# Key tiles of the second batch transposed ahead and stored in a conformer kernel

## The chip, the cores and the metric

One core of a Trainium2 chip. The metric is the device time of one execution in microseconds (us); the kernel before is given by the median of three runs.

## The reference

A conformer block over two batches of 4000 tokens with 512 features, in bf16:

```python
h = layernorm(x);  x1 = x + 0.5 * (silu(h @ w_ff1_a) @ w_ff1_b)
h = layernorm(x1); q, k, v = h @ w_q, h @ w_k, h @ w_v
p = softmax(q @ k^T / sqrt(512))              # every token of a batch against all of that batch
x2 = x1 + (p @ v) @ w_o
h = layernorm(x2) @ w_pw1; h = h[..., :D] * sigmoid(h[..., D:])
h = depthwise_conv3(h, dw); h = (h - mean) / sqrt(var + 1e-5)      # over all 8000 tokens
x3 = x2 + silu(h) @ w_pw2
h = layernorm(x3); x4 = x3 + 0.5 * (silu(h @ w_ff2_a) @ w_ff2_b)
return layernorm(x4)
```

## The kernel before

The weights of q and k are folded into one matrix, and v and the output weights into another, so the normalized tokens `h` themselves serve as keys and as values. The first feed-forward stage writes them to the DRAM tensor `keysd`. Attention then reads them in two forms: `self.h[kt]`, a plain copy with 128 tokens on the partitions (for the values), and `self.hT`, the same 128 tokens transposed, with features on the partitions (for the scores). A transposed tile comes from one DMA transpose (`key_queries`). A batch has 32 key tiles (`KT`), of which the last holds the 32 leftover tokens four times (`tailsd`).

`attention` runs 16 groups `g` of up to 512 queries, eight for each batch, and in each group 32 steps `kt`, one for each key tile. The first group of a batch (`g` 0 and 8) computes its scores plainly, tile by tile (`scores`). The other groups take the tiles 2 to 29 in seven quads of four tiles (`score_quad`), with a scheme that multiplies seven half-size products in place of eight; it needs sums of key tiles, made once in the first group of a batch by `k_sums`, stored in `kfd`, and read back in each group by `k_stream` into a pair of buffers. The value products use the same scheme (`pv`), with sums stored in `v12d` and `v4d` and read back by `v_stream`.

Between the two batches the key tiles in SBUF are exchanged while groups 7 and 8 run (`keys_swap`). The value side of it is prepared during groups 1 to 5: every ten steps, `v_ahead` loads two tiles of the second batch into the buffer `vst`, forms sums on VectorE and stores `vst`, `v4d` and `v12d`; `v_back` loads them in group 8. The transposed key tiles come by 32 DMA transposes spread over groups 7 and 8.

The tail tile of 32 tokens is scored by `tail_scores`: sixteen small matmuls into PSUM bank 1, an exponential, a store to `pqd` and four loads into `ptail`, which is read at the start of the next group (`sum_tail`, `pv_rest`). Its step is 9 in all groups but the first. At steps 24 and 28 a pair of convolution products for the group before is made (`pair`, `conv_b`, `conv_a`, `pw1`), whose PSUM bank comes from a ring (`sbank`).

All instructions are recorded first and then ordered for each engine by a planner (`Plan`). It goes through the program in time with costs of its own and takes for each engine, of what is ready, the instruction that is due first; TensorE (PE) may be reordered by at most 8 us of its own work, the other engines run at most 16 us ahead. The result is one fixed list for each engine. All DMAs named here are in the list of SyncE (SP), and an instruction that waits there holds up those behind it. Two instructions that write the same buffer are ordered by it:

```python
def transpose(self, dst, src, reads, writes):
    k = self.S.dsems[16 + self.nxt("tr", 12)]
    return self.S.dma("SP", k, lambda e: e.dma_start_transpose(dst, src), reads=reads, writes=writes)
```

All instructions are recorded through one helper, so in the profile they nearly all have line 93; they are told apart by the tensors that they write and read (`xt<-v12d`). In these names the regions stand: `keys` holds `h` and `hT`, `xt` the residual tiles and the buffers of `kfd` and `v12d`, `wff` the weights and `vst`, `work` queries and small buffers, `sums` the exponentials, `s` and `y` the eight PSUM banks.

Of the kernel before, what the change touches and what calls it, by code (L numbers as in the profile page):

```python
# [6 lines left out]
BF16 = mybir.dt.bfloat16  # L7
# [5 lines left out]
B, T, D, F, KW = 2, 4000, 512, 2048, 3  # L13
# [3 lines left out]
TPC = 4  # L17
# [11 lines left out]
QUADS = 7  # L29
HC, HD, HF = CHUNK // 2, D // 2, FC // 2  # L30
KT = -(-T // 128)
REST = T % 128
DC = D // 128
# [6 lines left out]
def width(c):  # L40

    return CHUNK if c % TCB < TCB - 1 else T - (TCB - 1) * CHUNK
# [11 lines left out]
def tile_rows(c, ti):  # L54

    if c % TCB < TCB - 1 or ti < TPC - 1:
        return slice(0, TILE)
    lo = c // TCB * HALF
    return slice(lo, lo + TAIL)
# [491 lines left out]
class Conformer:  # L551
# [35 lines left out]
    def memory(self):  # L587
        nc = self.nc
# [54 lines left out]
        at = [8192 + t % self.CONV_SLOTS * 4096 if t < self.NBESIDE else 20480 + (t - self.NBESIDE) * 4096  # L643
              for t in range(NCK)]
# [60 lines left out]
        self.hq = A.view(2048, QUADS * 2048).rearrange("p (q u r e j k) -> p q u r e j k", q=QUADS, u=2, r=2, e=2, j=2)  # L705
        self.kfd = nc.dram_tensor("kfd", [B, QUADS, 128, 1536], BF16, kind="Internal").ap()
        self.b_kfd = [[Buf("kfd") for _ in range(QUADS)] for _ in range(B)]
        self.vhd = nc.dram_tensor("vhd", [PAIRS, 128, 2 * D], BF16, kind="Internal").ap()
        self.v4d = nc.dram_tensor("v4d", [PAIRS, 128, HD], BF16, kind="Internal").ap()
        self.v12d = nc.dram_tensor("v12d", [B, PAIRS, 128, 2 * HD], BF16, kind="Internal").ap()  # L710
# [1224 lines left out]
    def v_ahead(self, i, step):  # L1935
# [9 lines left out]
        else:  # L1945
            self.store(self.vhd[i], x, b_x, [self.b_vhd[i]])
            self.store(self.v4d[i], f1, b_1, [self.b_v4d[i]])
            self.store(self.v12d[1][i], f2, b_2, [self.b_v12d[1][i]])

    def v_back(self, j, which):  # L1950
        p = self.group(j)
        i, k = p[0], p[-1] + 1
        if which:
            self.load(self.V4[:, i:k], self.v4d[i:k].rearrange("n p d -> p n d"), self.b_V4[i:k], reads=self.b_v4d[i:k])
        else:
            self.load(self.hv[:, i:k].rearrange("p n k e d -> p n (k e d)"), self.vhd[i:k].rearrange("n p d -> p n d"),
                      self.b_h[2 * i:2 * k], reads=self.b_vhd[i:k])
# [92 lines left out]
    def attention(self, old, hook):  # L2050

        for g in range(NCK):
            W, plain = width(g), g % TCB == 0
            for kt in range(KT):
                if plain:
                    self.ring = [0, 1, 2]
                else:
                    self.ring, self.rings["S"] = list(self.ASIDE.get(kt, (0, 1))), 0
                if plain and kt < KT - 1 or kt < 2 or kt == KT - 2:
                    ps, b_ps = self.scores(g, kt, None if plain else self.bank((0, 2)[kt] if kt < 2 else 0))  # L2060
                    if kt < KT - 2:
                        self.exp_pair(g, kt, ps, b_ps)
                    else:
                        self.act(self.P30[:, 0:W], ps[:, 0:W], AF.Exp, [b_ps], [self.b_P30], scale=SCALE)
                elif not plain and kt < KT - 2:
                    self.score_quad(g, *divmod(kt - 2, 4))
                if g == 0 and kt < 2:
                    self.pop(old // 2 if kt == 0 else old - old // 2)
                if kt == (9 if g else 21):
                    self.tail_scores(g)  # L2070
                if g:
                    self.units_late(g - 1, kt)
                self.units(g, kt)
                self.next_queries(g, kt, 9 if g else 0)
                hook(g, kt)
                self.forms(g, kt)
                self.keys_swap(g, kt)
                self.tick()
# [122 lines left out]
    def keys_swap(self, g, kt):  # L2201

        at = g * KT + kt
        if g == 0:
            steps = [(1, n) for n in range(5)] if kt == 3 else []
            j, r = divmod(kt + 1, 4)
            if 1 < j < GROUPS:
                steps += {0: [(j, 0)], 1: [(j, 1)], 2: [(j, 3)], 3: [(j, 2), (j, 4)]}[r]
            for j, n in steps:
                self.v_here(j, n)  # L2210
            if kt in (26, 27):
                self.v_rest(kt - 26)
        i, r = divmod(at - KT - 4, 10)
        if 0 <= i < PAIRS:
            for n in {0: (0,), 4: (1, 2), 5: (3, 4), 8: (5,)}.get(r, ()):
                self.v_ahead(i, n)
        if TCB - 1 <= g <= TCB:
            at -= (TCB - 1) * KT
            for k in range(KT):
                if (6 + k * (2 * KT - 12) // KT if k < KT - 1 else KT - 12) == at:  # L2220
                    self.key_queries(1, k)
            for j in range(GROUPS):
                if at == KT + 3 + j:
                    self.v_back(j, 0)
                if at == KT + 14 + j:
                    self.v_back(j, 1)
            if at in (KT + 11, KT + 12):
                self.key_values(1, KT - 2 + at - KT - 11)
            if at in (KT + 18, KT + 19):
                self.v_rest(at - KT - 18)  # L2230
# [138 lines left out]
            th, b_th = (self.thl[jj], self.b_thl[jj]) if t == NCK - 1 else (self.thh[k], self.b_th[k])  # L2369
            self.act(th[:, 0:W], ps[:, 0:W], AF.Sigmoid, [b_ps], [b_th])  # L2370

    def conv_a(self, t, jj):

        ps, b_ps = self.pw1(t, jj)
        k, gs, W = jj % 2, t % 2, width(t)
        th = self.th[k][:, 0:W]
        lo = 1 + self.EDGE * (t == NCK - 1)
        out = self.G[gs][:, jj, lo:lo + W]
        wr = [self.b_G[gs][jj], self.b_Gl[gs][jj], self.b_Gr[gs][jj]]
        if t == NCK - 2 and jj >= self.KEEP:  # L2380

            asb, b_asb = self.asb[jj % 3], self.b_asb[jj % 3]
            th = self.thh[k][:, 0:W]
            self.act(asb, ps[:, 0:CHUNK], AF.Copy, [b_ps], [b_asb], scale=2.0)

            def gate(eng):
                ways = {e: lambda e: e.tensor_tensor(out=out, in0=asb, in1=th, op=ALU.mult) for e in (eng, {"DVE": "POOL", "POOL": "DVE"}[eng])}
                self.S.either(ways, [b_asb, self.b_th[k]], wr)
                self.halo_left(t, jj)
                self.halo_right(t, jj)  # L2390

            return gate
        elif t == NCK - 1:
            self.S.op("DVE", lambda e: e.scalar_tensor_tensor(
                out=out, in0=ps[:, 0:W], scalar=2.0, in1=self.thl[jj][:, 0:W], op0=ALU.mult, op1=ALU.mult),
                reads=[b_ps, self.b_thl[jj]], writes=wr)
            return
        else:
            self.S.op("DVE", lambda e: e.scalar_tensor_tensor(
                out=out, in0=th, scalar=1.0, in1=ps[:, 0:W], op0=ALU.add, op1=ALU.mult),  # L2400
                reads=[b_ps, self.b_th[k]], writes=wr)
        self.halo_left(t, jj)
        self.halo_right(t, jj)

    def pw1(self, t, cb):
        ps, b_ps = self.sbank()
        n, W = TPC if width(t) == CHUNK else TPC - 1, width(t)
        if t == NCK - 1:
            moves = [(ps[:, 0:W], self.lin[:, :, 0:W])]
        else:  # L2410
            moves = [(ps[:, 0:n * TILE].rearrange("p (t k) -> p t k", t=n),
                      self.lnT[0][:, 0:n, :, 0:TILE].rearrange("p t c k -> p c t k"))]
            if n < TPC:
                moves.append((ps[:, n * TILE:W], self.lnT[0][:, n, :, tile_rows(t, n)]))
        for out, x in moves:
            for cc in range(DC):
                self.mm(out, self.Wp1[:, cc, cb * 128:(cb + 1) * 128], x[:, cc], cc == 0 and out is moves[0][0], cc == DC - 1,
                        [self.b_Wp1] + self.b_lnT[1 if t == NCK - 1 else 0], b_ps, skip_group_check=True)
        if t < NCK - 1:
            self.touch(ps, b_ps, W)  # L2420
        return ps, b_ps
# [207 lines left out]
    def program(self, any_score):  # L2629
        i = self.i  # L2630
# [99 lines left out]

        tail = NCK - 2

        def pair(t, jj):
            self.conv_b(t, jj)
            self.after(1, lambda: self.conv_a(t, jj))
            if t:
                self.after(3, lambda: self.taps_beside(t - 1, jj))

        here, there = ((22, 27), (3, 8)) if any_score else ((24, 28), (3, 5))

        def att_hook(g, kt):
            if g == 0 and kt == 8:
                self.load(self.Wp1, i["w_pw1"].rearrange("(c p) f -> p c f", p=128), [self.b_Wp1])
            if kt in here and (0 <= g - 1 < tail or g - 1 == tail and here.index(kt) < self.KEEP):
                pair(g - 1, here.index(kt))
            if 0 <= g - 2 < tail and kt in there:
                pair(g - 2, 2 + there.index(kt))
            if g == 0 and self.rest:
# [140 lines left out]
        for k in range(2):  # L2889
            pair = (2 * k, 2 * k + 1)  # L2890
            for ti in pair:
                self.ln_stats(0, sl, ti, x, ((), (), self.b_mv[sl][0:2], self.b_sh[sl][0:2])[ti])
            for ti in pair:
# [4 lines left out]
                 reads=self.b_mv[sl][two] + [self.b_neghalf], writes=self.b_rs[sl][two])  # L2898
# [16 lines left out]
        for ti in all_t:  # L2915
            ps, b_ps = banks[ti]
# [110 lines left out]
```

## Time and profile before

| | |
|---|---|
| median of 3 runs | 1886.56 us (1885.83 to 1886.96) |
| the profiled execution | 1887.44 us, of which its span is 1883.5 us |
| PE busy | 1861.0 us (99%), 15388 matmuls |
| VectorE (DVE) busy | 1485.6 us (79%) |
| ScalarE (ACT) busy | 1336.3 us (71%) |
| GpSimd (POOL) busy | 141.1 us (7%) |
| DMA | 231.50 MB, mean 123 GB/s |
| DMA transposes of keys | 62 from `keysd`, 2 from `tailsd` |

The span runs from the first to the last instruction; what the execution takes beyond it (3.9 us) lies around it. PE busy is the time covered by matmuls, so a gap in it is time in which no matmul was in the array. Attention lies between about 426 and 1400 us of the span.

### The profile page before, as it was taken

The numbers are of one execution on the slowest core, as the hardware profiler recorded it, in microseconds if no ns is written. First come the engines' busy times: TensorE is split into PE (matmuls) and PEld (weight loads), VectorE is DVE, ScalarE is ACT, GpSimd is POOL, SyncE is SP. The second block draws the span as 40 slices with busy tenths as digits, with TensorE's granted clock in tenths as the row PEclk, the third lists the DMA queues.
The fourth block names the chain that finished last, engine by engine and source line by source line (L and its number), as shares of the span: only waits on it lengthen the run. The fifth ranks groups of instructions, "written<-read, shape, count | busy, mean of one in ns | idle before, by whom it ended". The sixth has DMA issues, their size and how long they took to land.

```text
span 1883.5 us, 39160 instructions
## 1 busy us (share of the span) xinstructions
PE 1861.0 (99%) x15388; PEld 1441.9 (77%) x15388; DVE 1485.6 (79%) x3189; ACT 1336.3 (71%) x2421; POOL 141.1 (7%) x301
## 2 busy tenths in 40 slices
PE   9999999999999999999999999999998999999998
PEld 5888888866777777777677777777764888888886
DVE  7889999868668777776777677768768889889885
ACT  5778777755666777777667677777667787777774
POOL 1000000000000000000000000000011000000010
PEclk9999999999999999999999999999999999999999
DMA  7333344196545555348954444444365222221211
GB/s 196 89 85 90 81 113 107 60 271 208 168 142 150 166 167 164 109 127 174 226 149 132 128 124 114 123 137 125 105 197 163 66 59 78 70 55 46 64 32 55
DMA packets 325012, 231.50 MB, mean 123 GB/s; under 512 B 204179, under 2 KB 295638, under 8 KB 324566
## 3 DMA queue, kind: packets, MB, share of 16 engines
q1 hardware_dynamic: 324294, 228.68, 44.4%
q8 instruction: 123, 2.02, 0.4%
q14 instruction: 67, 0.55, 0.1%
q10 hardware_dynamic: 528, 0.26, 0.0%
HBM read 128.44 MB, written 55.79 MB: 98 GB/s over the span
## 4 chain that ended last, share of the span: by engine, by line
PE 93%; ACT 3%; DVE 2%; DMA 1%; issue 0%; SPq 0%; POOL 0%; DVEq 0%; ACTq 0%
PE s L93 47%; PE y L93 46%; ACT work L93 1%; DVE work L93 1%; DMA work<-work 1%; ACT sums L93 1%; ACT xt L93 0%; ACT keys L93 0%; DVE keys L93 0%; DVE wff L93 0%; SPq L93 0%; DVE xt L93 0%; DVE s L93 0%; ACT s L93 0%; DVE sums L93 0%
## 5 line engine op out<-in xcount | busy, mean ns | idle before, releaser
L93 ACT ACTIVATE sums<-s 128x512 bf16<-128x512 f32 (+2 forms) x494 | 287.4, 585 | 158.8 <-PE s L93 157.8
L93 DVE TENSOR_TENSOR sums<-sums 128x512 bf16<-128x512 bf16 (+3 forms) x528 | 201.8, 400 | 102.2 <-ACT sums L93 90.8
L93 ACT ACTIVATE keys<-s 128x512 bf16<-128x512 f32 (+2 forms) x284 | 165.3, 587 | 140.4 <-PE s L93 114.5
L93 PE MATMUL y<-work,keys 128*128 128x256 bf16 x1920 | 244.7, 273 | 0.0
L93 PE MATMUL s<-work,keys 128*128 128x256 bf16 (+5 forms) x1456 | 225.2, 292 | 0.4 <-ACT sums L93 0.3
L93 ACT ACTIVATE work<-xt,work 128x512 bf16<-128x512 bf16 x268 | 202.7, 785 | 10.2 <-DVE work L93 8.5
L93 PE MATMUL y<-wff,keys 128*128 128x256 bf16 (+3 forms) x1592 | 209.2, 276 | 0.1
L93 PEld LDWEIGHTS y<-work,keys 128*128 128x128 bf16 x1920 | 187.9, 98 | 25.1
L93 PE MATMUL y<-sums,keys 128*128 128x256 bf16 (+1 forms) x1440 | 202.1, 270 | 0.0
L93 PE MATMUL s<-sums 128*128 128x256 bf16 x1296 | 194.4, 273 | 0.0
L93 DVE TENSOR_TENSOR keys<-keys 128x1024 bf16<-128x1024 bf16 (+2 forms) x262 | 170.0, 663 | 25.8 <-ACT keys L93 20.4
L93 PE MATMUL y<-work,wff 128*128 128x256 bf16 (+2 forms) x1116 | 184.0, 292 | 0.0
L93 PEld LDWEIGHTS y<-wff,keys 128*128 128x128 bf16 (+1 forms) x1592 | 151.2, 98 | 32.4 <-issue 3.3
L93 DVE BATCH_NORM_STATS2 work<-xt 128x6 f32<-128x512 bf16 x251 | 165.9, 682 | 4.5 <-DMA xt<-in_x_dram 3.8
L93 PEld LDWEIGHTS y<-sums,keys 128*128 128x128 bf16 x1440 | 139.3, 98 | 24.5 <-DVE sums L93 0.3
L93 PEld LDWEIGHTS s<-work,keys 128*128 128x128 bf16 (+1 forms) x1456 | 119.4, 97 | 47.8 <-issue 4.7
L93 POOL TENSOR_TENSOR work<-work 128x4 f32<-128x4 f32 (+3 forms) x107 | 92.0, 862 | 808.4 <-DVE work L93 806.0
L93 PE MATMUL y<-sums,xt 128*128 128x256 bf16 (+1 forms) x960 | 139.7, 270 | 2.6 <-DMA xt<-v12d 1.9
L93 PEld LDWEIGHTS s<-sums 128*128 128x128 bf16 x1296 | 126.7, 98 | 20.0
L93 PE MATMUL s<-work,wff 128*128 128x512 bf16 (+5 forms) x668 | 140.2, 345 | 1.7 <-ACT work L93 1.1
L93 PE MATMUL s<-work 128*128 128x512 bf16 (+4 forms) x565 | 137.9, 374 | 2.4 <-DVE work L93 1.7
L93 PEld LDWEIGHTS y<-work,wff 128*128 128x128 bf16 x1116 | 108.2, 98 | 29.7
(144 smaller groups left out, 3217.4 us busy)
## 6 DMA issues: line engine op xcount, KB each, us to landing
xt<-kfd SPq DMA_DIRECT2D x98, 384.0 KB, 3.2
xt<-v12d SPq DMA_DIRECT2D x105, 256.0 KB, 3.1
xd<-xt SPq DMA_DIRECT2D x28, 512.0 KB, 3.4
xt<-xd SPq DMA_DIRECT2D x28, 512.0 KB, 4.1
out_dram<-xt SPq DMA_DIRECT2D x14, 512.0 KB, 2.9
xt<-in_x_dram SPq DMA_DIRECT2D x13, 512.0 KB, 4.1
dcvd<-wff SPq DMA_DIRECT2D x48, 128.0 KB, 2.0
keys<-dcvd SPq DMA_DIRECT2D x12, 512.0 KB, 3.8
```

Of the source, the lines that this page charges most:

```text
L93: return getattr(eng, self.name)(*self.args, **self.kw)
```

## The change

Fourteen pairs of the second batch's key tiles (the tiles 2 to 29, the seven quads) are transposed ahead. In groups 1 to 5, after each of the first fourteen rounds of `v_ahead`, two DMA transposes write into the same buffer `vst`, and a store puts it into a new DRAM tensor `khd`. In groups 7 and 8 `k_back` brings each pair back by one plain load. The tiles 0, 1, 30 and 31 are still transposed in groups 7 and 8, the last of them later than before. The sums and stores of `v_ahead` move to earlier steps of their round of ten. `tail_scores` moves from step 9 to step 24 in all groups but the first, and `conv_a` at step 24 is given bank 1.

```diff
         self.b_kfd = [[Buf("kfd") for _ in range(QUADS)] for _ in range(B)]
+        self.khd = nc.dram_tensor("khd", [2 * QUADS, 128, 2 * D], BF16, kind="Internal").ap()
+        self.b_khd = [Buf("khd") for _ in range(2 * QUADS)]
...
+    def k_ahead(self, i, step):
+
+        if step == 0:
+            for r in range(2):
+                src, rd = self.key_source(1, self.quad_tiles(i // 2)[2 * (i % 2) + r])
+                self.transpose(self.vst[:, r * D:(r + 1) * D].rearrange("p (c k) -> p c k", c=DC), src, rd, [self.b_vst])
+        else:
+            self.store(self.khd[i], self.vst, [self.b_vst], [self.b_khd[i]])
+
+    def k_back(self, i):
+        k = self.quad_tiles(i // 2)[2 * (i % 2)]
+        b = [self.b_hT[t // TPC][t % TPC] for t in (k, k + 1)]
+        q, u = divmod(i, 2)
+        self.load(self.hq[:, q, u].rearrange("p r e j k -> p (r e j k)"), self.khd[i], b, reads=[self.b_khd[i]])
...
-                if kt == (9 if g else 21):
+                if kt == (24 if g else 21):
                     self.tail_scores(g)
...
         i, r = divmod(at - KT - 4, 10)
         if 0 <= i < PAIRS:
-            for n in {0: (0,), 4: (1, 2), 5: (3, 4), 8: (5,)}.get(r, ()):
+            for n in {0: (0,), 2: (1, 2), 3: (3, 4), 5: (5,)}.get(r, ()):
                 self.v_ahead(i, n)
+            if i < 2 * QUADS and r in (6, 9):
+                self.k_ahead(i, r - 6)
...
-                if (6 + k * (2 * KT - 12) // KT if k < KT - 1 else KT - 12) == at:
-                    self.key_queries(1, k)
+                if (6 + k * (2 * KT - 12) // KT if k < KT - 1 else KT + 6) == at:
+                    if k < 2 or k > KT - 3:
+                        self.key_queries(1, k)
+                    elif k % 2:
+                        self.k_back((k - 2) // 2)
...
-    def conv_a(self, t, jj):
+    def conv_a(self, t, jj, bank=None):
 
-        ps, b_ps = self.pw1(t, jj)
+        ps, b_ps = self.pw1(t, jj, bank)
...
-    def pw1(self, t, cb):
-        ps, b_ps = self.sbank()
+    def pw1(self, t, cb, bank=None):
+        ps, b_ps = bank or self.sbank()
...
-        def pair(t, jj):
+        def pair(t, jj, bank=None):
             self.conv_b(t, jj)
-            self.after(1, lambda: self.conv_a(t, jj))
+            self.after(1, lambda: self.conv_a(t, jj, bank))
...
-                pair(g - 1, here.index(kt))
+                pair(g - 1, here.index(kt), self.bank(1) if kt == 24 else None)
```

## The prediction

> **What bounds the kernel now.** I read the page first, then the waits of PE, then the busy times by stage, and last the instructions around the worst stretch.
>
> ```profile
> span 1883.5 us, 39160 instructions
> PE 1861.0 (99%) x15388; PEld 1441.9 (77%) x15388; DVE 1485.6 (79%) x3189; ACT 1336.3 (71%) x2421; POOL 141.1 (7%) x301
> ```
>
> PE is the bound. The change removes no matmul from it, so it can only act on time in which PE stands still, 22.5 us in the whole span. The waits of PE, longest first in total, say how much of that belongs to DMAs (total, times, longest):
>
> ```profile
> PE s L93 <- ACT s L93: 2.9, 4, 0.9
> PE y L93 <- DMA xt<-v12d: 1.9, 2, 1.7
> ...
> PE s L93 <- DMA work<-work: 0.3, 1, 0.3
> ```
>
> Together 2.2 us of waits end with a DMA, 1.9 us of them with the stream of value sums. Where this happens is seen from the busy times by stage (time, PE, PEld, DVE, ACT, POOL, clock, DMA share, GB/s): groups 1 to 5, the exchange of the keys, and the second batch's groups behind it.
>
> ```profile
> 455.00:760.00 305.00, 303.58 (x2491) 228.43 (x2490) 227.48 (x521) 207.70 (x406) 19.00 (x53) 1.00 0.56 162
> 850.00:950.00 100.00, 96.91 (x767) 66.26 (x765) 71.13 (x176) 65.32 (x131) 6.87 (x20) 1.00 0.86 196
> 960.00:1300.00 340.00, 339.71 (x2803) 255.88 (x2801) 251.20 (x538) 246.16 (x480) 23.44 (x79) 1.00 0.44 123
> ```
>
> PE loses 3.1 us in the 100 us of the exchange, against 1.4 in 305 us and 0.3 in 340 us elsewhere, and the DMA engines are busy for 0.86 of it. What SP does there is seen in the order of time (start, duration, instruction), with PE's stop beside it:
>
> ```profile
> 871.71 0.58 SPq L93 DMA_DIRECT2D xt<-kfd  x1
> 872.33 2.50 SPq L93 DMA_TRANSPOSE keys<-keysd  x2
> 874.87 0.58 SPq L93 DMA_DIRECT2D xd<-xt  x1
> 875.49 0.43 SPq L93 DMA_DIRECT2D xt<-v12d  x1
> 875.97 1.63 SPq L93 DMA_TRANSPOSE keys<-keysd  x1
> 877.64 5.27 SPq L93 DMA_TRANSPOSE work<-work  x4
> ```
>
> ```profile
> 880.44 0.35 PE L93 MATMUL y<-sums,xt 128*128 128x208 bf16 x2 [1.68 <-DMA xt<-v12d]
> ...
> 884.38 1.89 PE L93 MATMUL s<-work,wff 128*128 128x512 bf16 x8 [0.34 <-DMA work<-work]
> ```
>
> SP issues without a pause. The load of `v12d` leaves at 875.49, behind key transposes, and PE waits for it until 880.44; the transposes of the row sums (`work<-work`) follow, and PE waits for them too. So the stretch is bound by SP's queue, and the change empties just this queue.
>
> **What leaves the exchange.** Durations on SP (min/median/max ns), for transposes and plain copies of the same 128 KB:
>
> ```profile
> L93 SPq DMA_TRANSPOSE keys<-keysd x62: 1188/1264/2619, 209.0 to 937.2; - x62
> L93 SPq DMA_DIRECT2D keys<-keysd x32: 336/472/1378, 381.0 to 915.3; - x32
> ...
> L93 SPq DMA_DIRECT2D wff<-keysd x15: 383/432/577, 456.9 to 729.0; - x15
> ```
>
> DMAs by issue, KB and median us to landing, in the exchange (850 to 950 us):
>
> ```profile
> xt<-kfd SPq DMA_DIRECT2D x4, 384.0 KB, 3.6
> ...
> keys<-keysd SPq DMA_TRANSPOSE x26, 3.3
> keys<-vhd SPq DMA_DIRECT2D x1, 256.0 KB, 4.4
> ```
>
> 28 transposes of about 1.26 us, 35 us on SP, go from groups 7 and 8, and 14 loads of about 0.45 us, 6 us, come: 29 us of SP's time are freed in about 100 us. In SP's list of the changed program no run of key transposes stands between one `v12d` load and the next in group 7. What the wait is worth: at the least nothing, if the load stays late for another reason; at the most the 3.1 us lost in the whole stretch. I take the 2.2 us of the two DMA rows, since ACT and DVE, which end the other small waits, do no less work than before.
>
> Here a rule of the Trainium skill speaks against the change: the page Advanced Engine Details and Errata (X-Bar Transpose (TRN2)) has it that transposing DMAs are as fast as regular ones. The trace differs on SP (1.264 against 0.472 us) and agrees on landing (3.3 us for a transpose, 3.6 for a `kfd` load). By the rule SP would be freed of 6 us in place of 29, and the sum below would lose its gain and be 1.5 us above the time before.
>
> **What comes to groups 1 to 5.** The transposes are not saved, they move, and 14 stores are added: in SP's list, each round of ten steps now is load, four sums on DVE, store of `vhd`, transpose, transpose, store of `khd`, next load, each waiting for the landing of the one before, since all use the one buffer `vst` (the second transpose waits for the first, as both write it). The same view for 455 to 760 us:
>
> ```profile
> wff<-keysd SPq DMA_DIRECT2D x15, 256.0 KB, 3.2
> vhd<-wff SPq DMA_DIRECT2D x15, 256.0 KB, 3.8
> ...
> work<-work SPq DMA_TRANSPOSE x30, 2.5
> ```
>
> and, from the order of time, the one round of before in which DVE had to wait for its load:
>
> ```profile
> 595.68 0.38 SPq L93 DMA_DIRECT2D wff<-keysd  x1
> ...
> 599.22 0.62 DVE L93 TENSOR_TENSOR wff<-wff 128x256 bf16<-128x256 bf16 x2 [0.79 <-DMA wff<-keysd]
> ```
>
> A `work<-work` transpose has the same 128x512 elements, so the loop is 3.2 + 3.8 + 2.5 + 2.5 + 3.8 (the store of `khd` like that of `vhd`) = 15.8 us, and four sums of 0.31 us make it 17.0 us. The period follows from the store of the tail's scores, once in each group:
>
> ```profile
> L93 SPq DMA_DIRECT2D pqd<-wff x16: 320/466/1261, 444.8 to 1361.6; - x16
> ```
>
> From step 21 of group 0 to step 9 of group 15 are 468 steps in 916.8 us, 1.96 us each, so a round is 19.6 us. The loop fits, with 2.6 us to spare, and SP waits in it. Queued behind these waits are the loads of `kfd` and `v12d`, on which PE depends. They have room: a buffer comes free six or seven steps (12 us) ahead of its next use, and landing takes 3.2 to 3.6 us.
>
> DVE has less room. It takes its sums in a fixed place, and DVE's list is now tighter behind the load. I laid the landing medians along SP's list, with PE at full pace: before, every load lands ahead of the place of its first sum; after, it lands behind it in 9 of 15 rounds, by up to 2.9 us and by about 11 us in all. This is an estimate from the lists and the rows above. On PE this costs between 0 and 11 us. The nearest row is the wait of 0.79 us shown above, the one of this kind; PE went on through it:
>
> ```profile
> 575.00:600.00 25.00, 25.00 (x197) 18.14 (x195) 20.50 (x49) 18.89 (x39) 1.40 (x6) 1.00 0.45 116
> 600.00:625.00 25.00, 25.00 (x215) 19.16 (x215) 19.93 (x47) 17.45 (x35) 2.64 (x5) 1.00 0.54 175
> ```
>
> DVE is busy for 227.48 of 305 us, so a quarter of its time can take such waits. Since some of them are three times as long as that one, I take 1.5 us.
>
> **Edits at nothing.** `k_back`: the first pair is asked for in group 7 and used at step 2 of group 8; the last comes at step 21 and is used at step 28, seven steps (13.7 us) against 4.4 us of landing; cover gone, PE waits for the landing. The tail's scores at step 24 leave eight steps (15.7 us, somewhat less in a batch's last group, whose queries are fewer) for this chain:
>
> ```profile
> 543.11 0.33 SPq L93 DMA_DIRECT2D pqd<-wff  x1
> ...
> 544.56 2.43 SPq L93 DMA_DIRECT2D wff<-pqd  x4
> ```
>
> Store at 543.1, the last of the four loads issued at 547.0, and with a landing of 3.6 us, the longest median above for a load of `xt`, in place at 550.6: 7.5 us, with as much again for waits on SP. Bank 1 at step 24 now takes the tail and then `conv_a`, at step 9 it is relieved of the same. One small matmul is added (`touch` on bank 1, below 0.1 us), and three copies change between ACT and DVE. The planner's lists differ in order all through attention, hardly behind it: this moves PE's stops by as much as one stage shows, 1.4 us to either side; I take 0.
>
> **Sum.** −2.2 + 1.5 = −0.7 us on the profiled execution of 1887.44 us: 1886.7. The median lies 0.9 us below the profiled execution: 1885.9 us. 0.2%, 3.8 us, is about what a measurement of this kernel can tell from no change.
>
> **Rivals.** *Slower: DVE's waits reach PE.* Place: the first sum of each round in groups 1 to 5. If each of the 11 us falls on PE, because scores wait for DVE's adds behind it, the time is 1886.6 − 2.2 + 11 = 1895.4. It decides from the point at which over 6 of the 11 us arrive (2.2 + 3.8). For it: five waits are over 1 us, and the landing in a crowded stage is longer (3.3 against 2.5 for a transpose), which would also take the loop of 17.0 us near its 19.6. Against it: the 0.8 us that cost nothing. Chance 0.35.
>
> *Faster.* All of the exchange's 3.1 us go, DVE's waits are taken by its idle quarter, and the new order also avoids the 1.4 us of 455 to 760 us: −4.5, 1882.0. For it: SP's queue is the one thing out of line in the exchange. Against: ACT and DVE end part of those stops. Chance 0.24.
>
> *No gain.* The load of `v12d` is late in any case, since the four `work<-work` transposes of 5.27 us and the second batch's values stay where they are: 1886.6 + 1.5 = 1888.1. Chance 0.11.
>
> **Numbers.** The forecast has 0.30; with the case without gain, 0.41 lies within 0.2%. Its own range is 1882.8 to 1889. The range of all reaches from 1880.5 (the faster case and 1.5 us of order) to 1896 (the slower case); beyond it lies a lag of SP's whole loop, or a stop at a place that the trace before does not show.
>
> **What would show it.** Right: no wait of PE on `xt<-v12d` near 880 us, over 99% PE busy between 850 and 950, the SP list there with pauses; DVE waiting for `wff<-keysd` 5 to 11 us in groups 1 to 5, and PE's loss there within 1.5 us of before. Wrong: PE losing over 5 us between 455 and 760 us (the slower rival), rounds longer than ten steps (the loop as pace), or `v12d` still late in group 7 (no gain).

## The result and the profile after

The changed kernel takes 1889.89 us (median of 13 runs, 1888.39 to 1894.72) against 1886.11 us of the kernel before on the same chip (13 runs, 1884.55 to 1887.56). The ratio is 1.0026 with a 95% interval of 1.0018 to 1.0033: 0.26% slower, where 1885.9, a little faster or no change, had been forecast. The interval is narrower than the 0.2% that the prediction took for what can be told from no change. The profiled execution took 1890.28 us.

The page after, its span and its engines:

```profile
span 1886.2 us, 39264 instructions
PE 1861.8 (99%) x15389; PEld 1441.4 (76%) x15389; DVE 1461.5 (77%) x3192; ACT 1306.3 (69%) x2418; POOL 133.0 (7%) x301
```

The span is 2.7 us longer: PE stands still for 24.4 us in place of 22.5, and its busy time grew by 0.8 us (1861.0 before). Where it stands still is seen from the busy times by stage (time, PE, PEld, DVE, ACT, POOL, clock, DMA share, GB/s), in the stretches that the prediction showed:

```profile
455.00:760.00 305.00, 299.69 (x2435) 224.62 (x2433) 221.71 (x515) 202.86 (x400) 17.27 (x53) 1.00 0.66 181
850.00:950.00 100.00, 98.75 (x788) 68.80 (x786) 69.72 (x174) 67.73 (x143) 6.57 (x22) 1.00 0.73 213
```

The exchange of the keys got better: PE loses 1.25 us in its 100 us, 3.09 before. Groups 1 to 5 got worse: 5.31 us in 305, 1.42 before. No wait of PE ends with a DMA any more. The waits of PE between 455 and 760 us (total, times, longest):

```profile
PE s L93 <- DVE s L93: 3.1, 6, 1.4
PE s L93 <- ACT s L93: 0.9, 2, 0.7
PE y L93 <- DVE sums L93: 0.7, 2, 0.4
```

They are waits for DVE and ACT. The waits of DVE and of SP's queue in the same stretch:

```profile
DVE wff L93 <- DMA wff<-keysd: 5.3, 6, 1.5
```

```profile
SPq L93 <- DMA wff<-keysd: 27.1, 20, 3.0
SPq L93 <- DMA khd<-wff: 16.7, 10, 3.5
```

DVE now waits six times for the load of a round; before it was once, for 0.8 us. The largest new stop, in the order of time (start, duration, instruction, idle time before it), first DVE and then PE:

```profile
504.47 0.69 DVE L93 TENSOR_TENSOR work<-work,xt 128x512 f32<-128x512 f32 x1
505.92 0.62 DVE L93 TENSOR_TENSOR wff<-wff 128x256 bf16<-128x256 bf16 x2 [0.76 <-DMA wff<-keysd]
506.64 0.29 DVE L93 TENSOR_TENSOR work<-wff 128x256 bf16<-128x256 bf16 x1
506.85 0.69 DVE L93 TENSOR_TENSOR s<-s,xt 128x512 f32<-128x512 f32 x1
```

```profile
505.62 0.60 PE L93 MATMUL s<-work,keys 128*128 128x256 bf16 x4
507.60 0.61 PE L93 MATMUL s<-xt,keys 128*128 128x256 bf16 x4 [1.37 <-DVE s L93]
```

The score add `s<-s,xt`, for which PE waits, stands in DVE's list behind three sums of the second batch's values, and the first of these waits for its load. Behind a wait of 0.76 us on DVE stands a stop of 1.37 us on PE. What of it is due to the sums, e13 below shows.

To tell the stages apart in every kernel I use one landmark for each group, the tail's value products at its start. The start of group 7, before and after:

```profile
838.22 0.28 PE L93 MATMUL y<-wff,keys 32*128 32x256 bf16 x1
```

```profile
844.21 0.28 PE L93 MATMUL y<-wff,keys 32*128 32x256 bf16 x1
```

So groups 1 to 6 end 6.0 us later than before, group 8 starts 4.2 us later (−1.8 in group 7), group 9 starts 3.3 us later (−0.9), group 14 starts 6.4 us later (+3.1), attention ends 4.7 us later and the last matmul 2.6 us later. The stretch from the start of group 1 to that of group 7, before and after (columns as above):

```profile
460.80:838.20 377.40, 375.12 (x3070) 281.86 (x3069) 279.91 (x631) 262.58 (x511) 24.91 (x70) 1.00 0.52 151
461.30:844.20 382.90, 376.69 (x3070) 281.97 (x3069) 277.92 (x633) 260.34 (x511) 22.21 (x70) 1.00 0.62 169
```

The same 3070 matmuls take 5.5 us longer: 3.9 us are more time standing still, and 1.6 us are more busy time at the same clock. Matmuls overlap in the rows: groups of four last 0.60 us and follow each other 0.44 us apart. A stop ends that overlap, so it costs a little more than its row says: the stop of 1.37 us above delays the next matmul by 1.54 us (505.62 + 0.44 to 507.60). Where a trace lacks some matmul records, the landmarks stand all the same. Below, "lag" is the landmark of a kernel less that of the kernel before, in the one profiled execution of each. The profiled execution of before lies 1.3 us above its median, so lags at the end come out a little lower than differences of medians. Some profiled executions lie further from their medians: those of e1, e13 and e15 are the fastest of their runs (1.7, 2 and 5.5 us below), that of e10 is 2.5 us above.

### The profile page after: what moved, and what is told of

Read it like the earlier page. It is cut to its first block, busy times and chain, and to the rows that moved or that the text cites. A ratio compares the mean times of both kernels' runs of the same rounds, so it can differ in the third digit from the quotient of the medians.

```text
span 1886.2 us, 39264 instructions
## 1 busy us (share of the span) xinstructions
PE 1861.8 (99%) x15389; PEld 1441.4 (76%) x15389; DVE 1461.5 (77%) x3192; ACT 1306.3 (69%) x2418; POOL 133.0 (7%) x301
## 4 chain that ended last, share of the span: by engine, by line
PE 91%; DVE 3%; DMA 2%; ACT 2%; issue 1%; SPq 0%; POOL 0%; DVEq 0%; ACTq 0%
PE s L93 46%; PE y L93 46%; DVE work L93 1%; DMA work<-work 1%; ACT work L93 1%; DMA wff<-keysd 1%; ACT sums L93 1%; DVE s L93 1%; DVE wff L93 0%; ACT wff L93 0%; DMA khd<-wff 0%; DVE xt L93 0%; DVE sums L93 0%; SPq L93 0%; DMA vhd<-wff 0%
## 5 line engine op out<-in xcount | busy, mean ns | idle before, releaser
L93 DVE TENSOR_TENSOR sums<-sums 128x512 bf16<-128x512 bf16 (+3 forms) x528 | 194.9, 398 | 74.0 <-ACT sums L93 69.3
L93 ACT ACTIVATE work<-xt,work 128x512 bf16<-128x512 bf16 x268 | 207.0, 786 | 8.4 <-DVE work L93 8.0
L93 PE MATMUL s<-xt,keys 128*128 128x256 bf16 (+1 forms) x816 | 124.4, 270 | 7.6 <-DVE s L93 5.0
```

Of the source, the lines that this page charges most:

```text
L93: return getattr(eng, self.name)(*self.args, **self.kw)
```

## The experiments

Three theories run through them. **A**: the transfers that were moved to groups 1 to 5, by their landing, cost the time. **B**: the order in which the planner now puts the work on PE, DVE and ACT costs it (B1: that it puts the sums ahead of score adds). **C**: any change of the plan moves the order by some microseconds, for better or worse.

| kernel | median us | before us | ratio (95%) | lag at group 7 | group 9 | end of attention |
|---|---|---|---|---|---|---|
| changed | 1889.89 | 1886.11 | 1.0026 (1.0018–1.0033) | 6.0 | 3.3 | 4.7 |
| e1 keys, no tail | 1887.43 | 1886.38 | 1.0009 (1.0000–1.0018) | 3.0 | 0.1 | 0.2 |
| e2 tail only | 1882.50 | 1886.38 | 0.9983 (0.9974–0.9992) | −0.3 | −2.8 | −4.0 |
| e3 gain only | 1883.52 | 1886.38 | 0.9985 (0.9976–0.9994) | 0.1 | −2.9 | −3.6 |
| e4 cost only | 1889.93 | 1886.38 | 1.0020 (1.0011–1.0029) | 4.0 | 3.3 | 2.5 |
| e5 halves | 1891.75 | 1887.06 | 1.0025 (1.0014–1.0036) | 7.8 | 5.0 | 6.3 |
| e6 round of 12 | 1892.73 | 1887.06 | 1.0036 (1.0022–1.0049) | 5.8 | 3.4 | 7.2 |
| e7 landing +1 us | 1889.73 | 1887.06 | 1.0016 (1.0007–1.0025) | 6.9 | 4.0 | 3.8 |
| e8 e5 and e6 | 1890.34 | 1887.06 | 1.0021 (1.0012–1.0031) | 5.2 | 2.8 | 4.3 |
| e9 order kept | 1889.46 | 1886.82 | 1.0014 (1.0005–1.0023) | 4.2 | 1.7 | 3.5 |
| e10 no spare | 1891.76 | 1886.82 | 1.0030 (1.0021–1.0039) | 9.6 | 6.6 | 8.6 |
| e11 before, no spare | 1899.80 | 1886.82 | 1.0067 (1.0053–1.0081) | 3.9 | 6.0 | 14.1 |
| e12 sums early | 1886.48 | 1886.82 | 0.9998 (0.9989–1.0007) | 0.1 | 1.0 | 1.0 |
| e13 sums yield | 1886.76 | 1887.24 | 1.0002 (0.9994–1.0011) | 2.7 | −0.3 | −1.0 |
| e14 ride, empty | 1883.78 | 1887.24 | 0.9980 (0.9971–0.9989) | 0.4 | −2.5 | −3.1 |
| e15 ride | 1940.17 | 1887.24 | 1.0282 (1.0268–1.0295) | 50.3 | 47.4 | 46.9 |
| e16 ride, tail | 1945.79 | 1887.24 | 1.0313 (1.0299–1.0326) | 56.8 | 54.2 | 57.0 |
| e17 before, sums yield | 1887.55 | 1887.18 | 1.0001 (0.9992–1.0009) | 0.0 | −0.3 | −0.1 |
| e18 e1, sums yield | 1886.05 | 1887.18 | 0.9995 (0.9987–1.0004) | 2.5 | −0.4 | −1.0 |

### The change taken apart

**e1**, the changed kernel with the tail scores back at step 9, key tile 31 at its old time, no bank for `conv_a`:

```diff
-                if kt == (24 if g else 21):
+                if kt == (9 if g else 21):
-                if (... if k < KT - 1 else KT + 6) == at:
+                if (... if k < KT - 1 else KT - 12) == at:
```

> The changed kernel with the tail's scores back at step 9, the last key tile back at its old time and no bank named for conv_a: the key tiles are transposed ahead, and that is all. Theory (the round's loop of five landings holds up DVE's first sum): groups 1 to 6 still lose about 5 us against before, DVE waits some 5 us for wff<-keysd, the time is 1889 to 1890 us. Rival 1 (the tail at step 24 is what costs): 1884 to 1886, with no loss in groups 1 to 6. Rival 2 (the planner's new order by itself): anywhere within 4 us, with PE's stops at other places and DVE not waiting for wff<-keysd.

**e2**, the kernel before with these edits alone (tail at step 24, bank 1, tile 31 at `KT + 6`):

> The kernel before with only the tail's scores at step 24, conv_a there in bank 1, and the last key tile transposed later. Theory: nothing of the loop is in it, so 1886 us within 1 us, groups 1 to 6 as before, and the wait for v12d near 880 us stays. Rival 1 (the tail costs): 1889 to 1890. Rival 2 (order alone): a difference of over 2 us to either side without a new kind of wait.

**e3**, the kernel before with the 14 loads in place of the 28 transposes, but nothing made ahead (the loads read stored values, so the second batch's scores are computed from other data):

```diff
-        self.load(..., self.khd[i], b, reads=[self.b_khd[i]])
+        self.load(..., self.vhd[i], b, reads=[self.b_vhd[i]])
```

> The gain by itself: no tile is transposed ahead and nothing is stored for it; groups 7 and 8 load 14 pairs of 256 KB all the same, from vhd, whose tiles are not transposed (so the second batch's scores are computed from other data), in place of 28 transposes. Tail and v_ahead as before. Theory: the exchange loses about 2 us less, groups 1 to 6 lose nothing, 1884 us. Rival (no gain in the exchange, the queue wasn't what held PE): 1886. Rival 2 (order alone): groups 1 to 6 change by over 2 us though nothing in them was edited.

**e4**, the keys transposed ahead and stored as in the change, but never read; the exchange as before:

```diff
-                    if k < 2 or k > KT - 3:
-                        self.key_queries(1, k)
-                    elif k % 2:
-                        self.k_back((k - 2) // 2)
+                    self.key_queries(1, k)
```

> The cost by itself: 28 transposes into vst and 14 stores to khd in groups 1 to 5 as in the changed kernel, khd is never read, and groups 7 and 8 transpose all tiles as before. Tail as before. Theory: groups 1 to 6 lose about 5 us as in the changed kernel, and the exchange loses its 3 us again: 1891 us (1890 to 1893). Rival 1 (the tail costs): 1886 to 1887. Rival 2 (order alone): no fixed sign, DVE not waiting for wff<-keysd.

The exchange by itself gives what the prediction took from it, and the work ahead by itself costs 4.0 us in groups 1 to 6 (3.0 in e1; about 5 had been expected of both). From the start of group 7 to that of group 9, e3 and e1 gain 2.9 us each and the changed kernel 2.7. Busy times by stage, e3 and then e2:

```profile
455.00:760.00 305.00, 303.56 (x2491) 228.41 (x2490) 227.28 (x521) 207.74 (x406) 19.00 (x53) 1.00 0.57 162
850.00:950.00 100.00, 99.23 (x788) 68.09 (x786) 71.93 (x176) 66.68 (x133) 7.43 (x23) 1.00 0.73 211
```

```profile
455.00:760.00 305.00, 303.92 (x2486) 229.57 (x2485) 226.49 (x523) 205.93 (x405) 16.80 (x53) 1.00 0.56 161
850.00:950.00 100.00, 99.10 (x787) 68.68 (x786) 70.05 (x173) 64.70 (x133) 6.45 (x20) 1.00 0.85 208
```

The surprise is e2. It still issues all its key transposes in the exchange, the DMA share there is still 0.85, and it loses 0.9 us of PE in that stretch instead of 3.1. SP's queue in e2 around the stop of before, in the order of time:

```profile
871.48 1.26 SPq L93 DMA_TRANSPOSE work<-work  x1
872.79 1.52 SPq L93 DMA_DIRECT2D xt<-v12d  x1
874.36 3.81 SPq L93 DMA_TRANSPOSE work<-work  x3
878.22 0.58 SPq L93 DMA_DIRECT2D xt<-kfd  x1
878.84 0.43 SPq L93 DMA_DIRECT2D xt<-v12d  x1
879.32 2.50 SPq L93 DMA_TRANSPOSE keys<-keysd  x2
```

The load of `v12d` at 872.79 now stands ahead of three of the four transposes of the row sums, and the next two key transposes behind them: PE waits for no DMA in this stretch. So another order of the queue removes the stop as well as an emptier queue does. The gains of e2 and e3 in the exchange are therefore for the most part the same microseconds: before lost 3.1 us there, and each of them leaves less than 1. No run has both edits without the keys ahead. Which of the three edits of e2 makes its gain was not tested. At 1882.50 us e2 is the fastest kernel of the study, faster than both.

### The loop of landings

The first theory behind the loss was the loop load, sums, store, transposes, store on the one buffer. Four kernels loosen it. **e5**: `vst` as two halves, so that the second transpose doesn't wait for the first. **e6**: rounds of 12 steps. **e8**: both. **e7**: the planner counts 1 us more to the landing of each DMA.

```diff
-        self.vst, self.b_vst = ..., W.buf("vst", 28672, 4 * D)
+        self.vst, self.b_vst = ..., [W.buf("vst", 28672 + n * 2 * D, 2 * D) for n in range(2)]
-        i, r = divmod(at - KT - 4, 10)
+        i, r = divmod(at - KT - 4, 12)
-                n.land = pipe - s + 1000
+                n.land = pipe - s + 2000
```

(The first edit is that of e5, the second of e6, the third of e7.)

> The changed kernel with vst recorded as two halves, so that the second transpose of a pair no longer waits for the landing of the first; the same transfers. Theory (the loop of landings holds up DVE): the loop is some 2.5 to 3.4 us shorter, DVE's waits for wff<-keysd fall from 5.3 us to under 2, groups 1 to 6 lose under 3 us in place of 6, and the time is 1885 to 1887 us. Rival 1 (the traffic and SP's issue time are what costs, whoever waits): as the changed kernel, 1889 to 1890. Rival 2 (the tail at step 24 together with the transposes costs on PSUM bank 1, not through the loads): groups 1 to 6 still lose 5 to 6 us with DVE's waits for wff<-keysd gone.

> The changed kernel with a round every twelve steps in place of ten (23.5 us in place of 19.6; the last round ends in group 6). The same transfers and the same waits within a round. Theory: the loop has 4 us more to end, the load of the next round is no longer held by the store of khd, DVE's waits fall to under 2 us, 1885 to 1887 us. Rival 1 (each transfer costs by itself): 1889 to 1890. Rival 2 (DVE is held because the planner believes loads to land sooner than they do, however long the round): DVE's waits stay near 5 us.

> The changed kernel with one constant of the planner changed: it believes every DMA to land 1 us later. Same instructions and transfers, other order. Theory (the place of DVE's first sum in its list is too close behind the load because the planner's belief is short): DVE's waits for wff<-keysd fall to under 2 us, and groups 1 to 6 lose 2 to 4 us less, 1885 to 1888 us. Rival 1 (traffic): 1889 to 1890. Rival 2 (order alone): a difference with no relation to DVE's waits.

> Both of the last two loosenings but not the planner's constant: two halves of vst, and twelve steps a round. Theory: no wait of DVE for wff<-keysd, groups 1 to 6 as before, the exchange's gain kept: 1881 to 1884 us, under the kernel before. Rival 1 (traffic): 1888 to 1890. Rival 2 (bank 1): groups 1 to 6 lose 3 us or more.

All four were expected to gain if the loop held up PE. None does: groups 1 to 6 lose 5.2 to 7.8 us. e7 takes DVE's wait away almost wholly (455 to 760 us), and loses 6.9 us:

```profile
DVE wff L93 <- DMA wff<-keysd: 0.2, 1, 0.2
```

So the time that DVE waits for its load isn't the measure of what PE loses, and a looser loop is no cure.

### Order or transfers

**e9** keeps every instruction of the changed kernel at its place on every engine and empties the transfers: the planner books them as before, the chip gets copies of four rows (second batch's scores from other data).

```diff
+                self.S.plan.dma(..., [lambda e: e.dma_start_transpose(...)], rd, [self.b_vst],
+                    real=[lambda e: e.dma_start(dst[0:4], src[0:4])])
```

> The changed kernel with every instruction of it at its place, the same order on every engine and queue, but with the transfers of the new work nearly empty: each of the 28 transposes ahead is a plain copy of four rows, each of the 14 stores of transposed keys is of four rows (the second batch's scores are computed from other data, which the loads in the exchange bring at full size). Theory A, the transfers themselves (their bytes, their landing, the load that waits behind them) cost the time: groups 1 to 6 lose under 2 us against before instead of 6, and the kernel is at about 1885. Theory B, the order in which the score adds, the sums and the other work of DVE and PE now stand costs it, whatever the transfers do: groups 1 to 6 still lose 4 us or more, and the kernel stays within 1.5 us of the changed one, 1888.5 to 1891.

**e10** and **e11**: the planner's 3 us of reserve for each transfer set to nothing, in the changed kernel and in the kernel before. **e12**: the kernel before with the sums at steps 2, 3 and 5, nothing else.

```diff
-    SPARE = 3000
+    SPARE = 0
```

> The changed kernel, with the 3 us that the planner takes off the due time of each transfer's work set to nothing. A round's chain holds six transfers, so 18 us of its 33 us of planned length go, and the chain is no longer overdue in every round. Theory B1, the overdue chain lets the sums of the second batch's values go ahead of the score adds on DVE: groups 1 to 6 then lose under 2.5 us instead of 6, and the kernel is at 1885 to 1887. Theory A, transfers: as the changed kernel, 1889 to 1891. Theory C, the order comes out a few us better or worse at any change of the plan: anything between 1884 and 1893, and the kernel before moves as much under the same edit.

> The kernel before with the same 3 us set to nothing, as a measure for the run above. Theory B1: the chain of the kernel before is not overdue, so little changes, within 1.5 us of before, 1885 to 1888. Theory C: it moves by 2 us or more either way.

> The kernel before with the four sums and the stores of each round put at steps 2, 3 and 5 of the round, as the change puts them, and nothing else of the change: no transposes ahead, the exchange as before. Theory A, transfers: within 1 us of before, 1885.5 to 1887.5. Theory B1, the sums at their early places ahead of score adds are enough: groups 1 to 6 lose 2 us or more, 1888 to 1890. Theory C: within 2 us of before either way.

e9 decides between A and B for the larger part. The compute instructions of PE, DVE and ACT stand in its trace in the same order as in the changed kernel's. Its "transposes" are short (min/median/max ns on SP), and between 455 and 760 us DVE waits for a round's load once, for 1.0 us, in place of six times; yet the stop near 505 us is there, at the same instruction (DVE, then PE):

```profile
L1960 SPq DMA_DIRECT2D wff<-keysd x28: 268/279/485, 470.4 to 740.1; - x28
```

```profile
506.12 0.62 DVE L93 TENSOR_TENSOR wff<-wff 128x256 bf16<-128x256 bf16 x2 [1.02 <-DMA wff<-keysd]
506.85 0.29 DVE L93 TENSOR_TENSOR work<-wff 128x256 bf16<-128x256 bf16 x1
507.06 0.69 DVE L93 TENSOR_TENSOR s<-s,xt 128x512 f32<-128x512 f32 x1
```

```profile
507.81 0.61 PE L93 MATMUL s<-xt,keys 128*128 128x256 bf16 x4 [1.64 <-DVE s L93]
```

The lag at group 7 is 4.2 us with empty transfers and 6.0 with real ones: 4.2 us belong to the order (with the short copies that are left in it), 1.8 to the transfers. The medians, each against its own before, say about the same: 2.6 us of 3.8. From the start of group 9 to that of group 14, where no transposes were moved to, the changed kernel loses another 3.1 us and e9 3.5, so this too is the order; e1, with the tail at its old step, loses 0.1 there. e12 shows that the early steps of the sums are not it: without the keys the same steps cost nothing. e10 and e11 show that the reserve is no handle: e10 is slower still, where B1 had 1885 to 1887, and the kernel before itself loses 13 us by it. They also show C to be real: an edit of the plan alone can be worth over 10 us.

### The sums behind the score adds, and an order that doesn't know the transfers

**e13** puts the due times of the four sums 20 us later in the plan, so that they stand ahead of other work only where DVE would be idle. **e17** is the same edit in the kernel before, **e18** in e1.

```diff
+        for n in self.nodes:
+            n.late += n.low        # 20000 ns for the sums of v_ahead, else 0
         free = {e: 0.0 for e in self.AFTER}
```

> The changed kernel, with the due times of the four sums of each round put 20 us later in the plan, so that a sum stands ahead of another DVE instruction only where DVE would else be idle. Theory B1, the sums placed ahead of score adds are what the order costs: groups 1 to 6 lose under 2 us, and the kernel is at 1884 to 1886. Theory C, the whole order comes out differently with every change of the plan, and none of it is due to the sums: groups 1 to 6 lose 3 us or more somewhere, or the total lies anywhere between 1884 and 1893.

> The kernel before with the sums' due times put 20 us later, as the run on the changed kernel had them. Its DVE waits once, for 0.8 us, for the load that the sums need, and its sums stand 6 to 10 us behind that load. Theory B1, the loss belongs to sums that stand where their load lands, ahead of score adds, in the crowded rounds: nothing to gain here, within 1.5 us of before, 1885.5 to 1888.5. Theory C, any such edit reorders to the good: 1 to 4 us faster, 1883 to 1886.

> The keys ahead and the loads in the exchange, the tail scores at their old step, and the sums put 20 us later in the plan. Theory B1: the loss of groups 1 to 6 falls from the 3.0 us of the same kernel without the edit to 0 to 1.5, the exchange gains its 2 to 3, and the kernel is at 1883.5 to 1886, 1.5 to 4 us below its 1887.4. Theory C: 1887 to 1890, the loss stays or moves elsewhere.

In the changed kernel the edit takes the loss of groups 1 to 6 from 6.0 to 2.7 us and the median from 3.8 us above its before to 0.5 below it (1886.76 against 1887.24). This lies between the expectations: B1 had under 2 us of loss, C 3 or more. In the kernel before the edit does nothing, as B1 expected, so it isn't a better order for any kernel. In e1 it takes 3.0 to 2.5, less than B1 expected. Where the gain comes from shows at a stop of the changed kernel near 613 us, DVE and PE:

```profile
608.10 0.62 DVE L93 TENSOR_TENSOR wff<-wff 128x256 bf16<-128x256 bf16 x2 [1.46 <-DMA wff<-keysd]
608.63 0.74 DVE L93 SCALAR_TENSOR_TENSOR xt<-s,work,xt 128x512 bf16<-128x512 f32 x1
...
612.80 0.69 DVE L93 TENSOR_TENSOR s<-s,xt 128x512 f32<-128x512 f32 x1
```

```profile
613.55 0.61 PE L93 MATMUL s<-xt,keys 128*128 128x256 bf16 x4 [0.87 <-DVE s L93]
```

and at the same place in e13, where no sum waits, two of the four stand behind the add, and PE goes on:

```profile
606.92 0.75 DVE L93 SCALAR_TENSOR_TENSOR xt<-s,work,xt 128x512 bf16<-128x512 f32 x1 [0.89 <-PE s L93]
...
610.29 0.29 DVE L93 TENSOR_TENSOR wff<-wff 128x256 bf16<-128x256 bf16 x1
...
611.30 0.69 DVE L93 TENSOR_TENSOR s<-s,xt 128x512 f32<-128x512 f32 x1
```

```profile
612.05 0.61 PE L93 MATMUL s<-xt,keys 128*128 128x256 bf16 x4
```

At the first stop, near 505 us, nothing is gained. With no sum ahead of the same score add, PE still waits 0.43 us for it, so by this comparison about 0.9 of the 1.37 us there belong to the sums and their wait. But the load is late even for the sums' later place, and the add behind the first sum makes PE wait 0.98 us more (DVE, then PE):

```profile
508.09 0.29 DVE L93 TENSOR_TENSOR wff<-wff 128x256 bf16<-128x256 bf16 x1 [1.99 <-DMA wff<-keysd]
508.30 0.68 DVE L93 TENSOR_TENSOR xt<-s,xt 128x512 f32<-128x512 f32 x1
```

```profile
506.16 0.61 PE L93 MATMUL s<-xt,keys 128*128 128x256 bf16 x4 [0.43 <-DVE s L93]
...
509.04 0.61 PE L93 MATMUL s<-xt,keys 128*128 128x256 bf16 x4 [0.98 <-DVE xt L93]
```

**e14** to **e16** ask the reverse: an order that was planned without the transposes and stores ahead, and the transfers put into SP's queue after the plan is made. e14 is that order without them (second batch's scores from stored values), e15 with them, e16 with the tail edits too. The compute instructions of PE, DVE, ACT and POOL stand in the same order in the traces of e14 and e15.

```diff
+        for n, e, s in best[1]:
+            while due and n.e == "SP" and (s >= due[0][0] or n.tag == "load"):
+                due.pop(0)[1]()          # a transpose or store, 3 or 8 us behind the round's stores
```

> The order for the next two runs, without the transposes and stores ahead: the sums at steps 2, 3 and 5, the 14 loads in the exchange (here of the second batch's stored values in place of its keys, so its scores are computed from other data), the tail scores at their old step. Every theory: the exchange gains about 2 to 3.6 us as it did with this alone; by theory C the rest of the order moves the total by up to 4 us, so 1881 to 1888.

> The same order of every instruction on PE, DVE, ACT and POOL as in the run without them; the 28 transposes and 14 stores are put into the DMA queue of SP after the plan is made, 3 and 8 us behind the stores of each round's values, and the exchange loads the keys. Theory A, the transfers themselves cost: 4 us or more above the run without them. Theory B or C, the order costs and the transfers next to nothing: under 2 us above it.

> The whole of the change (tail scores at step 24, bank 1, key tile 31 later, too), with the transposes and stores put into the queue after the plan as above. Theory B or C: the order is that of a kernel without them, so groups 1 to 6 lose under 2 us, the exchange gains 2 to 3 us, and the kernel is at 1881 to 1885, the tail's own gain included. Theory A: 1888 to 1891 as the changed kernel.

e14 behaves like e3. e15 and e16 refute what B and C expected here: the same order with the transfers in it loses 50 us more in groups 1 to 6. Theory A had the sign (4 us or more for e15, 1888 to 1891 us for e16), and nobody the size. The waits of DVE in e15 between 455 and 760 us, and one of them beside the queue that made it:

```profile
DVE wff L93 <- DMA wff<-keysd: 32.9, 9, 5.9
```

```profile
480.75 0.38 SPq L93 DMA_DIRECT2D wff<-keysd  x1
```

```profile
483.56 0.62 DVE L93 TENSOR_TENSOR wff<-wff 128x256 bf16<-128x256 bf16 x2 [5.37 <-DMA wff<-keysd]
```

```profile
484.84 0.61 PE L93 MATMUL s<-xt,keys 128*128 128x256 bf16 x4 [4.14 <-DVE xt L93]
```

The load leaves at 480.75, since it has to follow the store of the transposed keys; DVE, whose list has the sums early, stands for 5.37 us until 483.56, and PE for 4.14. Not all of the 50 us is standing still. Groups 1 to 6 of e15, and in them the time just behind that stop (columns as above, the clock third from the end):

```profile
460.90:888.50 427.60, 387.59 (x3069) 286.38 (x3069) 279.83 (x630) 263.34 (x512) 24.49 (x70) 0.97 0.53 151
486.00:489.20 3.20, 3.20 (x14) 1.66 (x12) 1.62 (x5) 0.61 (x2) 0.00 (x0) 0.51 0.42 124
```

PE stands still for 40.0 us there, 37.7 more than before, and is busy 12.5 us longer with as many matmuls: behind the long stops the granted clock is half for some microseconds. A and B thus look like two sides of one cause. The transfers lengthen a round: the order made without them pays for that at the load (with this place in the queue; others weren't tried), and the planner, which knows of them, makes another order and pays for that, at about a tenth of the price. The transposes and the loads of the 15 rounds in the changed kernel (min/median/max ns, first and last start):

```profile
L93 SPq DMA_TRANSPOSE wff<-keysd x28: 1188/1191/1669, 470.3 to 743.3; - x28
...
L93 SPq DMA_DIRECT2D wff<-keysd x15: 383/384/582, 457.8 to 750.7; - x15
```

From load to load that is 20.9 us a round ((750.7 − 457.8) / 14), against 19.4 before (456.9 to 729.0); PE's own loss explains 0.4 us of it at most. e9, with its transfers empty, has 20.6 (457.8 to 746.0): the pace is the planner's.

## Why the prediction was wrong

**Right.** The bound: PE's work didn't change, and the difference lies in its stops and the overlap that they end. The exchange: PE's 2.2 us of waits for DMAs, 2.0 of them between 850 and 950 us, are gone, and the stage gives −2.7 us where −2.2 was forecast; SP's queue there has pauses. That the emptier queue was needed for it is not shown: e2 gains 2.5 us there with all its transposes. The expected 99% of PE was missed narrowly (98.75), by 1.2 us of waits for DVE. Transposes cost SP more than copies after the change too: 1191 ns for one of 128 KB in groups 1 to 5, against 384 ns for a load of 256 KB. The rule of the Trainium skill that speaks against this (page Advanced Engine Details and Errata, X-Bar Transpose (TRN2), that transposing DMAs are as fast as regular ones) holds for the landings alone: medians of 3.1 us for these transposes and 3.0 us for these loads. The waits of the edits at nothing: `k_back`, bank 1 and the tail's chain at step 24 put no wait for a DMA on PE. The kind of DVE's waits, though at half their size: six rounds, up to 1.5 us, 5.3 us in all, where 9 rounds, 2.9 and about 11 us were estimated.

**Wrong: the step "I take 1.5 us" for groups 1 to 5.** It had bounds of 0 and 11 and took its value by the row of a DVE wait of 0.79 us during which PE went on. The changed kernel loses 6.0 us there at the start of group 7, e4 4.0 and e1 3.0. The row was of the wrong kind: it tells what a wait costs where the waiting instruction stands ahead of nothing urgent. After the change three sums and their wait stand ahead of a score add, and PE stops for 1.37 us behind a wait of 0.76. The slower rival named the place ("because scores wait for DVE's adds behind it"), but it priced the wait alone; most of the cost is the order, 4.2 us of 6.0 with empty transfers, and e7, almost without the wait, lost 6.9 us.

**Wrong: "planner's lists differ in order … I take 0".** Its ±1.4 us was the loss of PE in one stage of before, which measures how good that order is and not how far another may be from it. The runs put the size at 4 us to the better (e2, with half of it or more in the exchange) and 13 to the worse (e11). Nor was the new order without effect later: groups 9 to 13 lose 3.1 us, group 14 to the end of attention gives back 1.7 and the part behind attention 2.1.

**Wrong: the tail's edits at nothing.** Their transfers do no harm, but the edits move the order: by themselves they gain 3.9 us (e2), and on top of the keys ahead they cost 2.7 (the medians of the changed kernel and of e1, each against its own before).

**Wrong in its size: the round of 17.0 us in 19.6.** The landings came to 14.7 us (3.0, 2.7, 3.1 twice and 2.8) where 15.8 was taken, but the round became 20.9. The links are not what fills it, since it is 20.6 with empty transfers: each link also has its place in SP's list, and that is where the plan put it.

**The sum** by what was measured: +6.0 ahead of the exchange, −2.7 in it, +3.1 to group 14, −1.7 to the end of attention and −2.1 behind it make the +2.6 us at the last matmul; the profiled executions differ by 2.8 us and the medians by 3.8. The forecast had terms for the first two parts alone, and that the others nearly cancel is luck.

**Open.** About 2.5 us of the loss in groups 1 to 6 stay when the sums yield (e13, e18). Over 1 us of them falls near 505 us (group 2 starts 1.6 and 1.3 us late in these two), in e13 at the late load; which of the reordered instructions carry the rest was not settled. Nor is it settled why the tail's new step, harmless alone (−0.3), raises the loss of the keys from 3.0 to 6.0 us; that the sums' yielding takes it away (2.7 against 2.5) suggests, and no more, that it comes about through the same DVE list. Open, too, are the 3.1 us of groups 9 to 13, which neither e1 (0.1) nor e2 (0.6) loses.

## What to carry to other kernels

Work that is moved from a crowded stage into an idle one is not free where fixed lists are planned around it: price the instruction that waits by what stands behind it in its list, not by how long it waits. Before a transfer is moved away, see whether another order of two neighbours in the queue removes the same stop; here moving the tail's sixteen small matmuls of each group, with a bank and one key tile, gained 3.9 us, and moving 28 transposes lost 1.0 without these edits and 3.8 with them. Where a planner makes the order, run the change with its transfers emptied and with its order frozen: the two runs tell the order's cost from the transfers'.

## What was not expected of the hardware

One constant of the planner is worth 13 us, with PE's clock granted in full (1.00) in attention in both kernels. A stop can cost more than its length: in e15 PE's clock is granted at 0.51 from 486.0 to 489.2 us, behind the stop of 4.14 us, and four matmuls of 128x512 take 1.91 us there against 1.03 ahead of the stop. The stops of up to 2.3 us in e11 show no such drop. A DMA transpose of 128 KB holds SP's list for 1.19 us at the least, in an uncrowded stage as in a crowded one, while a copy of four rows (4 KB) holds it for 0.28 us and a load of 256 KB for 0.38. At a DMA share of 0.66 in place of 0.56, the landing of stores of 256 KB did not get longer (2.7 us against 3.8).
